# A spectral filter and a Mish network, gated, on one core: W's column copies on VectorE, four small first loads, a 128-column last piece and a new written order

## The chip, the core and the metric

The kernel runs on one core of a Trainium2 chip. Its engines work at the same time and meet only at semaphores: TensorE (PE) multiplies into PSUM, which has eight banks of 512 float32 columns; VectorE (DVE) and ScalarE (ACT) work element by element and empty PSUM; GpSimd (POOL) can do small element work in SBUF; SyncE (SP) issues the loads and stores. The metric is the time of one execution on the device, in microseconds. Three runs of the kernel before gave a median of 133.03 (132.91 to 133.15).

## What is computed

The reference, cut to what matters:

```python
x = A_x                                             # [1, 2048, 512], bf16
g = sigmoid((x * gate_w).sum(-1, keepdims=True))    # one gate for each row
a = irfft2(rfft2(x) * (A_w_r + 1j * A_w_i))         # a 2-D spectral filter, bf16
h = x @ w1 + b1                                     # [2048, 512] @ [512, 1792]
b = (h * tanh(softplus(h))) @ w2                    # Mish, then [1792, 512]
return g * a + (1 - g) * b                          # both branches read the same x
```

## The kernel before, in words

All work is cut into some 490 small tasks with names. A string, `ORDER` (L343), lists them; each engine runs its own tasks in the order in which they stand there. `place` adds what has to be waited for: the data, the former users of a buffer, and, for every load on SP, the sixth load before it (`KOUT = 6`). A task that is an engine's next but has to wait holds up everything behind it on that engine. In an entry such as `m0_0::2`, 2 is the PSUM bank (of a pair, the first); an engine name between the colons chooses the engine of tasks that have several.

The tasks that matter here, by name:

- `warm` and `fl`: products of a constant, which compute nothing that is used. `warm` is one run of `NWARM` products of 256 columns (L525); each `fl` is two products of 128 columns (L533, L534).
- `x0`, `x2`, ... load tiles of x (128 rows of 512; `XP` says which tiles one load takes). `graw` loads the gate's weights to all partitions. `w1_*`, `w2_*`, `ldM*`, `ldG*` load weights and transform matrices, `wr*s*` and `wi*s*` the filter W, `xt*` x tiles transposed by the DMA. `tr0` to `tr3` transpose the first four tiles on PE (L582), and `evx*` copy these out of PSUM.
- the spectral branch: `bf` (sums and differences of x's halves, L595, DVE), `p` (L613, PE) with eviction `ep`, `d` (L628) with `ed`, `t` (L706) with `et`; the filter, `hp`, `p1`, `ad` (L725, L728, L732, all on DVE); the edge frequencies `c0`, `e1`, `xp`, `ead`, `e2`, `e3`, of which `e3` writes into all the data that the inverse transform reads; `it` (L788) with `eit`; `id` (L827) with `ec` and `ey`.
- W's preparation, for the real and the imaginary part (`wr`, `wi`) and each half of the frequencies (0, 1): four moves `wrm000` ... `wim111` (L657, L658), a copy of one column `wrc`, `wic` (L675), a copy to the other 64 partitions, negated for the imaginary part, `wrn`, `win` (L670 on DVE, L673 on ACT), and a small fill `wrz`, `wiz` (L679).
- the gate: `gt0` to `gt15` (L602, DVE) multiply x in place and sum; `zcl`, `ez` (a power on POOL, L689), `omg`, `gc` and others make factors of it.
- the network: `m0_0` to `m3_13` (L853), four products of 512 columns each, for one of four row blocks and one of fourteen column blocks; `h0_0` to `h3_13` apply bias and Mish on ACT (L858); `h3_*` write over W's staging buffer, so they wait for all of W's moves. `ev_b` makes the bias column. `n0_0` ... `n15_0` (L871) are fourteen products each, `ip` adds the spectral branch (L879 for tiles 8 to 15, L897 for 0 to 7), `o` scales by 1 - g (L885 on ACT, L888 on DVE), `fin` adds the rest for tiles 0 to 7 (L901), `out` stores. The last tile, 15, is cut into two column pieces.

Of the kernel before, what the change touches and what calls it, by code (L numbers as in the profile page):

```python
# [340 lines left out]


ORDER = """  # L343
tab x2 ones braw cRF x0 fl9::0 w1_0 ident warm::1 bf2_0 fl6::2 tr2::3 w1_2 x4 bf2_1 evx2:dve x12 tr3::4 evx3:act w1_6 bf0_0 bf0_1 fl2::5 graw::0 p2::6
tr0::0 x8 tr1::1 w1_10 fl0::2 p3 cFD evx0:act p0::4 tr_b::3 p1 ep0:act xt7 evx1:dve m0_0::2 ev_b xt6 xt4 xt5 ep2:dve m0_1::0 m0_5::1 h0_0 ebase wr0s0
wr0s2 h0_5 bf4_0 m0_2::3 m0_3::4 h0_2 bf4_1 p4::6 wr0s1 bf12_0 bf12_1 p5 p6::1 p7 ep6:dve m0_4::5 m0_8::3 h0_3 wi0s0 ep4:act wi0s2 p14::6 gt7 p15
p12::1 p13 gt13 h0_8 h0_4 wi0s1 ep14:act m0_6::4 ep12:act bf8_1 ldM0 m0_7::3 bf8_0 p10::6 p11 gt8 xt11 ep10:act m0_13::5 gt1 h0_6 gt3 gt9 p8::1 p9
ep8:dve m0_11::6 h0_7 h0_11 gt15 m0_10::7 d0::3 gt12 h0_13 h0_10 d1 d8::1 m1_6::6 h1_6 xt10 h0_1 m1_5::5 h1_5 ldM1 m1_11::7 h1_11 d9 ed8:act ed0:dve
d12::3 d4::5 d13 xt8 gt0 gt4 d5 ed4:act m0_12::0 ed12:dve xt9 wrm010:dve d14::1 d15 wi1s0 ldM3 d2::3 d3 m1_13::7 ed14:act ed2:act h1_13 ldM2 m1_0::5
wrm000:dve h1_0 h0_12 d10::1 wr1s0 d11 ed10:act m1_1::6 m1_9::3 h1_1 wr1s1 wi1s1 m1_4::4 h1_4 xt14 h1_9 gt10 m1_3::7 h1_3 d6::1 xt13 d7 ed6:act  # L350
m1_8::5 t0::36 gt14 gt6 h1_8 gt2 et00:act xt12 et01:act m0_9::0 h0_9 m1_10::1 h1_10 gt5 xt15 t1::42 et11:act et10:act m2_9::6 h2_9 m2_12::7 h2_12
wrm001:dve m2_1::0 m2_4::1 wrm011:dve m1_2::2 h1_2 gt11 h2_4 wrc0:dve m1_7::3 h1_7 wim000:dve w2_5 m2_0::4 h2_0 wim001:dve w2_0 wrn0:dve ldG2 wrz0:dve
m2_7::5 m2_6::6 wim010:dve m2_5::7 h2_6 h2_5 m2_8::2 wim011:dve wic0:pool h2_1 m2_11::1 h2_7 win0:dve h2_8 h2_11 wiz0:pool hp00_1::1 c00 t2::36 hp00_0
hp01_1::2 hp01_0 c01 et21:act p1_00 m2_2::0 h2_2 p1_01 ad_01 hp11_0::0 hp11_1 p1_11 m1_12::5 h1_12 hp10_0::2 m2_3::2 hp10_1 ad_11 wrm100:dve et20:act
wrm110:dve h2_3 wrm111:dve wrm101:dve wim111:dve wrc1:dve t3::60 m2_13::5 et31:act m2_10::3 h2_13 wim101:dve wim110:dve wim100:dve edge et30:act
wic1:pool win1:act m3_8::4 h3_8 wrn1:dve zcl ez wrz1:pool w2_10 p1_10 ad_10 ad_00 m3_13::2 m3_1::0 wiz1:dve hp30_1::0 hp30_0 m3_12::1 ldG3 c02
m3_10::5 h3_10 h3_13 ldG0 m3_2::6 h3_12 h2_10 m3_3::7 m3_0::4 h3_0 hp20_0::2 m3_6::5 c03 p1_30 m3_11::2 hp31_1::1 m3_4::1 hp20_1 p1_20 ezb hp31_0
e1::3 p1_31 ad_31 m3_9::4 h3_1 m3_5::0 xp20::1 h3_11 xp21 n2_0::2 ad_20 h3_2 h3_6 h3_4 ad_30 h3_5 xp1::2 zt::6 ead::0 hp21_0::1 n1_0::5 hp21_1 p1_21
h3_9 zte zw ad_21 inv m3_7::1 ez1 e2::0 ldG1 n0_0::4 h3_7 e3 it4_0::0 it4_1 h3_3 rft omg o1_0:act zr o2_0:dve o0_0:act it0_0::6 it0_1 eit0:dve
it1_0::2 it1_1 eit4:dve n3_0::5 o3_0:dve it6_0::6 it6_1 eit6:act it7_0::0 it7_1 rfs eit7:act n9_0::4 eit1:dve it3_0::6 it3_1 it2_0::0 it2_1 it5_0::2  # L360
it5_1 n6_0::5 eit5:act eit2:act eit3:dve id4::6 id8::2 id9 o6_0:dve ec8:dve:2 ey8_1 ey8_0 id12::0 id13 ec12:act:0 id5 ec4:act:1 ey4_0 ey4_1 n5_0::5
o5_0:dve id6::2 id7 ec6:dve:2 id2::6 id3 ey6_1 ey12_0 ip9_0 n8_0::5 ey6_0 ec2:act:1 ip8_0 ey2_1 id14::2 ey12_1 id15 ey2_0 id0::0 id1 ec14:dve:2
o9_0:dve id10::6 o8_0:act out9 id11 ec0:dve:0 ec10:dve:1 ey10_0 n13_0::5 ey14_0 ip13_0 ey0_0 n15_256::4 ey14_1 ip15_256 o15_256:dve out15_256
o13_0:act ey10_1 ey0_1 n4_0::5 ip4::2 o4_0:act gc fin4 ip5::3 fin5 n7_0::4 ip6::6 o7_0:dve fin6 out5 ip0::7 fin0 ip2::0 ip7::1 fin7 ip1::5 fin1 out1
n14_0::2 ip3::3 ip14_0 o14_0:act out14 out7 n10_0::4 ip10_0 n11_0::6 ip11_0 o11_0:dve n12_0::7 ip12_0 n15_0::1 fin3 ip15_0 o10_0:act fl1::5 fin2 out3
fl8::2 fl4::4 o12_0:act out11 out13 fl7::6 o15_0:act out15_0 fl5::3 fl3::0
"""


def _build(nc, A_x, A_w_r, A_w_i, B_x, B_w1, B_b1, B_w2, gate_w, out, merge=8, xtp=XTP, NWARM=13):  # L370
    cs = _build_consts()
# [7 lines left out]
    G = _Graph(3)  # L379
    es = ExitStack()  # L380
    with es:
# [260 lines left out]
        for ri, (dstv, nm) in enumerate(((Wr, "wr"), (Wi, "wi"))):  # L642
            dp = t_bf + t_tr + t_gt if ri else []
            for fh in range(2):
# [27 lines left out]
                def f_dupa(e, f0=f0, dstv=dstv, sc=sc):  # L672
                    return e.activation(dstv[64:128, f0:f0 + 32, :], dstv[0:64, f0:f0 + 32, :], AF.Copy, scale=sc)  # L673

                G.add(f"{nm}c{fh}", [(g, 0.2, lambda e, dstv=dstv, f0=f0: e.tensor_copy(  # L675
                    out=dstv[0:64, f0:f0 + 32, 129], in_=dstv[0:64, f0:f0 + 32, 0])) for g in ("dve", "pool")],
                      "w", lock=True, reads=mv, writes=[(nm, fh, "c")])
# [1 line left out]
                G.add(f"{nm}z{fh}", [(g, 0.1, lambda e, dstv=dstv, ri=ri, f0=f0: e.memset(dstv[:, f0:f0 + 32, 0:1], 1.0 - ri)) for g in ("dve", "pool")],  # L679
                      "w", reads=[(nm, fh, "c")], writes=[wk])  # L680
# [164 lines left out]
        for c in range(NCH):  # L845
# [14 lines left out]

            for tl in range(4):
                t = 4 * c + tl
                for lo, hi in ([(0, 256), (256, 512)] if t == NT - 1 else [(0, 512)]):
# [13 lines left out]
                    if mg:  # L877
                        def f_ip(e, t=t, b=b, lo=lo, hi=hi):
                            return e.matmul(bank(b)[:, 0:hi - lo], RFs[:, t, :], yb[:, t, lo:hi], start=False, stop=True)  # L879
# [4 lines left out]
                    def f_oa(e, t=t, b=b, lo=lo, hi=hi):
                        return e.activation(bs[:, t, lo:hi], bank(b)[:, 0:hi - lo], AF.Copy, scale=omg[:, t:t + 1])  # L885
# [73 lines left out]
```

## Time and profile before

| | us |
|---|---|
| median of three runs | 133.03 |
| the profiled execution | 132.57 |
| its span, first to last instruction | 130.5 |
| PE busy | 124.8 |
| DVE busy | 95.3 |
| ACT busy | 69.5 |
| POOL busy | 6.2 |

The profile is of one execution. Its span leaves out about 2 us around the instructions. A row of the chain of waits gives a start, a length and what ran; a row of the groups gives line, engine, operation, tiles, shapes and count, then busy time, the mean of one in ns, and the engine's idle time before with what ended it. A matmul's listed length contains its fill and drain, which the next overlaps; what one costs in a run is the distance of two starts.

### The profile page before, as it was taken

How to read it: one execution, taken by the hardware profiler on the slowest of the kernel's cores; microseconds unless marked ns; L12 is line 12 of the kernel's file. 1: busy time of each engine (PE TensorE's matmuls, PEld its weight loads, DVE VectorE, ACT ScalarE, POOL GpSimd, SP SyncE). 2: the span in 40 equal slices, each digit the busy share in tenths (PEclk: the TensorE clock that was granted, in tenths of full speed). 3: DMA queues.
4: the chain of work that ended last, by engine and by line, in shares of the span. 5: the costliest groups of instructions: out<-in, count | busy, mean ns of one | idle time of the engine just before them, and what ended most of it. 6: DMA issues, size and time to landing. Idle time of an engine off the chain costs nothing.

```text
span 130.5 us, 2641 instructions
## 1 busy us (share of the span) xinstructions
PE 124.8 (96%) x1097; PEld 68.6 (53%) x1114; DVE 95.3 (73%) x162; ACT 69.5 (53%) x96; POOL 6.2 (5%) x12
## 2 busy tenths in 40 slices
PE   7999999999999999996999999999999999999994
PEld 5856555755554455442444454666456554444463
DVE  0758999799979999996999987734899964630230
ACT  4358798999996699959990240532212102022021
POOL 2000000000010000095000000000000000000000
PEclk9999999999999999999999999999999999999999
DMA  3899999999999791078100027000000200223024
GB/s 111 259 387 304 270 178 197 122 361 166 402 119 170 189 358 64 5 224 263 75 0 0 0 52 245 1 0 5 0 0 5 80 20 0 80 80 121 0 89 178
DMA packets 17143, 16.90 MB, mean 130 GB/s; under 512 B 7596, under 2 KB 14252, under 8 KB 17068
## 3 DMA queue, kind: packets, MB, share of 16 engines
q1 hardware_dynamic: 16960, 16.66, 53.6%
q8 instruction: 9, 0.15, 0.5%
q10 hardware_dynamic: 172, 0.07, 0.2%
q14 instruction: 2, 0.02, 0.0%
HBM read 13.05 MB, written 2.10 MB: 116 GB/s over the span
## 4 chain that ended last, share of the span: by engine, by line
PE 65%; DVE 21%; issue 4%; ACT 3%; DMA 3%; POOL 2%; SPq 1%; DVEq 0%; ACTq 0%; POOLq 0%
PE ps L871 37%; PE ps L853 15%; DVE tmp L725 4%; PE ps L788 3%; ACT rA L673 3%; DMA rA<-in_A_x_dram 3%; PE ps L613 3%; PE ps L827 2%; DVE rA L602 2%; DVE rA L658 2%; DVE rA L657 2%; DVE rW L657 2%; DVE rW L658 2%; DVE rC L728 1%; PE ps L879 1%
## 5 line engine op out<-in xcount | busy, mean ns | idle before, releaser
L853 PE MATMUL ps<-rX,w_sb 128*128 128x512 bf16 x215 | 49.5, 379 | 2.0 <-ACT rS L858 1.1
L853 PEld LDWEIGHTS ps<-rX,w_sb 128*128 128x128 bf16 x224 | 21.0, 98 | 24.8 <-ACT rS L858 1.6
L871 PE MATMUL ps<-w_sb,hs 128*128 128x512 bf16 x107 | 24.7, 379 | 0.4 <-DVE tmp L835 0.2
L885 ACT ACTIVATE rX<-ps,omg 128x512 bf16<-128x512 f32 (+1 forms) x9 | 5.9, 665 | 29.4 <-PE ps L879 23.6
L858 ACT ACTIVATE hs<-ps,b1f 128x512 bf16<-128x512 f32 x28 | 18.1, 698 | 4.1 <-PE ps L853 4.0
L871 PEld LDWEIGHTS ps<-w_sb,hs 128*128 128x128 bf16 x112 | 10.6, 98 | 12.0
L888 DVE TENSOR_SCALAR rX<-ps,omg 128x512 bf16<-128x512 f32 (+1 forms) x8 | 5.7, 716 | 14.1 <-PE ps L879 8.4
L512 ACT ACTIVATE rC<-ps 128x1024 bf16<-128x1024 f32 x13 | 13.4, 1078 | 0.6 <-PE ps L613 0.6
L871 PE MATMUL ps<-w_sb,rS 128*128 128x512 bf16 (+1 forms) x69 | 12.7, 336 | 0.2 <-issue 0.2
L871 PE MATMUL ps<-w_sb,rD 128*128 128x512 bf16 x54 | 12.6, 379 | 0.1
L858 ACT ACTIVATE rS<-ps,b1f 128x512 bf16<-128x512 f32 x14 | 8.5, 720 | 5.8 <-PE ps L853 5.8
L725 DVE TENSOR_TENSOR tmp<-rC,rA 64x1024 bf16<-64x1024 bf16 x16 | 10.9, 685 | 0.8 <-POOL rA L679 0.4
L602 DVE SCALAR_TENSOR_TENSOR rA<-rA,tmp 128x512 bf16<-128x512 bf16 x16 | 10.2, 684 | 0.2 <-DMA tmp<-in_gate_w_dram 0.2
L838 DVE TENSOR_TENSOR rA<-tmp,ps 128x512 bf16<-128x512 f32 x16 | 9.9, 680 | 0.1
L858 ACT ACTIVATE rD<-ps,b1f 128x512 bf16<-128x512 f32 x14 | 9.3, 708 | 1.2 <-PE ps L853 1.2
L732 DVE TENSOR_TENSOR rE<-rC,tmp 128x1024 bf16<-128x1024 bf16 x8 | 9.6, 1221 | 0.3
L871 PEld LDWEIGHTS ps<-w_sb,rS 128*128 128x128 bf16 x70 | 6.8, 98 | 5.6
L595 DVE TENSOR_TENSOR rB<-rA 128x1024 bf16<-128x1024 bf16 (+1 forms) x10 | 5.4, 582 | 5.3 <-DMA rA<-in_A_x_dram 5.1
L871 PEld LDWEIGHTS ps<-w_sb,rD 128*128 128x128 bf16 x56 | 5.4, 98 | 6.2
L512 ACT ACTIVATE rF<-ps 128x1024 bf16<-128x1024 f32 x4 | 3.9, 1023 | 6.6 <-PE ps L788 6.6
L901 DVE SCALAR_TENSOR_TENSOR rX<-ps,gcol,rX 128x512 bf16<-128x512 f32 x8 | 5.5, 742 | 2.1 <-ACT rX L885 2.1
L509 DVE CAST rF<-ps 128x1024 bf16<-128x1024 f32 x4 | 4.8, 1220 | 2.2 <-PE ps L788 2.2
(79 smaller groups left out, 120.2 us busy)
## 6 DMA issues: line engine op xcount, KB each, us to landing
w_sb<-in_B_w_dram SPq DMA_DIRECT2D x4, 512.0 KB, 6.5
rF<-c_m SPq DMA_DIRECT2D x4, 512.0 KB, 6.5
rB<-c_g SPq DMA_DIRECT2D x4, 512.0 KB, 6.7
out_dram<-rX SPq DMA_DIRECT2D x7, 256.0 KB, 2.1
rA<-in_A_x_dram SPq DMA_DIRECT2D x3, 512.0 KB, 6.8
w_sb<-in_B_w_dram SPq DMA_DIRECT2D x2, 640.0 KB, 6.0
rS<-in_A_w_r_dram SPq DMA_DIRECT2D x3, 257.0 KB, 7.1
rS<-in_A_w_i_dram SPq DMA_DIRECT2D x3, 257.0 KB, 5.8
```

The costliest lines, as they stand in the source:

```text
L512: return e.activation(o(), i(), AF.Copy)
L595: return e.tensor_tensor(out=xu[:, a:b_, uv, :], in0=x_sb[:, a:b_, 0:256], in1=x_sb[:, a:b_, 256:512], op=ALU.add if uv == 0 else ALU.subt ...
L602: t_gt.append(G.add(f"gt{t}", [("dve", 0.6, lambda e, t=t: e.scalar_tensor_tensor(out=x_sb[:, t, :], in0=x_sb[:, t, :], scalar=1.0, in1=tb ...
L725: return e.tensor_tensor(out=z3(z)[lo], in0=y3[hi], in1=wi3[hi], op=ALU.mult)
L732: return e.tensor_tensor(out=Yhq[:, q, h], in0=v(yv), in1=v(tb(z)), op=ALU.add)
L838: return e.tensor_tensor(out=yb[:, t:t + 2, 256 * h:256 * h + 256].rearrange("p t (i e) -> p t i e", e=2), in0=t4(z), in1=o4(bank(b, 1)), ...
L853: ins = e.matmul(bank(b), w1_sb[:, dt_, 128 * ft:128 * (ft + 1)], xT[:, c, dt_, :, :], start=(dt_ == 0), stop=(dt_ == 3))
L858: G.add(f"h{c}_{ft}", [("act", act(512, 1), lambda e, c=c, ft=ft, b=b: e.activation(hs[c][:, ft, :], bank(b), AF.Mish, bias=b1f[:, ft:ft + ...
L871: ins = e.matmul(bank(b)[:, 0:hi - lo], hs[c][:, ft, 128 * tl:128 * (tl + 1)], w2_sb[:, ft, lo:hi], start=(ft == 0), stop=(ft == NFT - 1 a ...
L885: return e.activation(bs[:, t, lo:hi], bank(b)[:, 0:hi - lo], AF.Copy, scale=omg[:, t:t + 1])
L888: return e.tensor_scalar(out=bs[:, t, lo:hi], in0=bank(b)[:, 0:hi - lo], scalar1=omg[:, t:t + 1], scalar2=None, op0=ALU.mult)
L901: return e.scalar_tensor_tensor(out=bs[:, t, :], in0=bank(b), scalar=gcol[:, t:t + 1], in1=bs[:, t, :], op0=ALU.mult, op1=ALU.add)
```

## The change

Six things change, all of them in the tasks and their order; what is computed stays.

- W's column copies and small fills can no longer be put on POOL. The copies may go to DVE or ACT; the fills are on DVE.
- The first four x tiles come in four loads of one tile instead of two loads of two, so each has its own pair of `bf` tasks, of 256 columns instead of 512.
- `NWARM` is 8 instead of 13; there are 13 fillers instead of 10.
- The last tile is cut into 128 and 384 columns instead of 256 and 256. `n15_128` and `n15_0` stand at the very end.
- `ORDER` is written anew, for all engines.
- In it the choice of engines differs: `win1` (before on ACT), `wic0` and the fills are on DVE, `wim101`, `wrm110`, `wic1` and `wrc1` on ACT.

```diff
-NFILL = 10
+NFILL = 13
-XP = ((0, 2), (2, 4), (4, 8), (8, 12), (12, 16))
+XP = ((0, 1), (1, 2), (2, 3), (3, 4), (4, 8), (8, 12), (12, 16))
...
-def _build(nc, A_x, A_w_r, A_w_i, B_x, B_w1, B_b1, B_w2, gate_w, out, merge=8, xtp=XTP, NWARM=13):
+def _build(nc, A_x, A_w_r, A_w_i, B_x, B_w1, B_b1, B_w2, gate_w, out, merge=8, xtp=XTP, NWARM=8):
...
-                G.add(f"{nm}c{fh}", [(g, 0.2, lambda e, dstv=dstv, f0=f0: e.tensor_copy(
-                    out=dstv[0:64, f0:f0 + 32, 129], in_=dstv[0:64, f0:f0 + 32, 0])) for g in ("dve", "pool")],
+                c_o, c_i = dstv[0:64, f0:f0 + 32, 129], dstv[0:64, f0:f0 + 32, 0]
+                G.add(f"{nm}c{fh}", [("dve", 0.2, lambda e, o=c_o, i=c_i: e.tensor_copy(out=o, in_=i)),
+                                     ("act", 0.2, lambda e, o=c_o, i=c_i: e.activation(o, i, AF.Copy))],
...
-                G.add(f"{nm}z{fh}", [(g, 0.1, lambda e, dstv=dstv, ri=ri, f0=f0: e.memset(dstv[:, f0:f0 + 32, 0:1], 1.0 - ri)) for g in ("dve", "pool")],
+                G.add(f"{nm}z{fh}", [("dve", 0.1, lambda e, dstv=dstv, ri=ri, f0=f0: e.memset(dstv[:, f0:f0 + 32, 0:1], 1.0 - ri))],
...
-                for lo, hi in ([(0, 256), (256, 512)] if t == NT - 1 else [(0, 512)]):
+                for lo, hi in ([(0, 128), (128, 512)] if t == NT - 1 else [(0, 512)]):
...
-                              reads=[("yb", t, h) for h in (0, 1) if lo <= 256 * h < hi] + ["RFs"], writes=[b])
+                              reads=[("yb", t, h) for h in (0, 1) if lo < 256 * h + 256 and 256 * h < hi] + ["RFs"], writes=[b])
...
-                    keys = [("bs", t, h) for h in (0, 1) if lo <= 256 * h < hi]
+                    keys = [("bs", t, lo)] if t == NT - 1 else [("bs", t, 0), ("bs", t, 1)]
```

The new order, in the parts that the prediction speaks of:

```diff
+fl8::0 tab x0 warm::1 ones ident fl7::2 fl0::3 x2 x1 bf2_1 x3 cRF w1_0 bf0_0 fl10::4 bf2_0 fl6::5 tr0::6 tr2::7 bf0_1 evx0:dve tr1::0 fl1::1 w1_2
+graw::0 x4 w1_6 x12 tr3::2 bf1_0 bf1_1 fl5::3 fl2::4 p0::5 bf3_0 p1 p2::3 evx2:dve w1_10 x8 braw tr_b::1 evx1:act bf3_1 p3 gt1 evx3:act m0_0::0 ev_b
+ep0:act gt3 ep2:act xt5 xt4 m0_1::7 bf4_0 bf4_1 h0_1 xt7 m0_4::2 xt6 h0_4 m0_5::5 h0_5 gt6 m0_2::6 h0_2 h0_0 m0_3::3 h0_3 gt4 bf12_1 p6::1 p7 m0_8::4
+p4::6 cFD p5 ep6:act xt10 h0_8 bf12_0 gt13 ep4:act m0_6::5 ldM0 m0_7::0 h0_7 p12::2 p13 ep12:act m0_12::1 gt12 h0_6 p14::6 wi0s2 p15 gt14 h0_12
...
+m1_10::3 h1_12 wim011:dve wic0:dve d4::4 d5 ed4:act xt15 h1_10 xt12 t0::06 et01:act m1_3::2 h1_3 ldM2 wi1s1 wi1s0 et00:act m2_8::4 ez win0:dve
+m2_11::5 h2_11 t1::62 wr1s0 et10:dve wr1s1 et11:act c01 m2_1::0 h2_1 w2_5 c00 wiz0 hp11_1::1 m2_13::1 w2_0 hp00_0::2 m1_6::5 h1_6 h2_13 hp11_0 hp00_1
+m1_2::2 h1_2 m2_10::3 m1_7::6 h1_7 ez1 w2_10 ldG2 m2_2::7 h2_2 h2_10 m1_11::0 wrm000:dve h1_11 m1_0::5 m2_4::1 omg ldM3 wrm001:dve t2::62 h1_0 ldG3
+et21:act et20:act m2_9::0 h2_9 m2_0::5 wrm011:dve wrm010:dve wrc0:dve h2_0 m3_3::2 hp10_1::0 hp10_0 ezb m2_5::3 h2_4 wrn0:dve wrz0 p1_00 wim101:act
+p1_10 ad_10 h2_5 m3_11::6 ad_00 m2_3::7 h2_3 wim110:dve m1_8::0 c02 h2_8 m1_1::5 h1_1 m2_7::1 h2_7 wrm110:act hp01_0::0 m3_4::3 wim100:dve hp01_1 h1_8
+p1_01 wim111:dve m3_8::7 m3_2::4 wrm101:dve m3_10::5 wrm111:dve wrm100:dve edge wic1:act win1:dve h3_8 h3_3 ldG0 ldG1 m3_1::1 h3_10 wiz1 h3_4 ad_01
+m3_5::0 h3_5 m3_12::7 wrc1:act hp20_0::2 m3_9::2 m3_7::5 h3_2 m3_0::3 h3_12 h3_0 wrn1:dve h3_11 h3_9 hp21_1::0 wrz1 p1_11 n0_0::0 hp20_1 h3_7 t3::36
+et31:act et30:act hp21_0 p1_21 ad_21 n3_0::2 o3_0:act p1_20 ad_20 m2_12::5 c03 e1::6 h3_1 ad_11 m2_6::7 h2_6 n1_0::3 o1_0:act xp20::0 xp21 xp1::2
+ead::1 e2::4 m3_13::2 hp31_0::0 hp31_1 p1_31 hp30_0::2 ad_31 m3_6::1 hp30_1 n2_0::6 h3_13 p1_30 ad_30 e3 o0_0:act h3_6 o2_0:dve it2_0::2 inv it2_1
...
+o14_0:act out14 out1 fin4 ip5::7 fin5 n13_0::0 ip12_0 o12_0:act ip3::4 fin3 out5 ip7::3 ip13_0 ip2::2 n15_128::5 ip15_128 o15_128:act n15_0::1 ip15_0
+fin2 out3 fl4::7 fin7 out7 o15_0:act o13_0:dve out13 fl9::6 fl12::4 out15_128 fl11::2 out15_0 fl3::3
```

More of the change, by code (lines that the diff above doesn't have):

```diff
@@ L343 @@
 ORDER = """
[L344 to L363, printed above, removed]
@@ new lines @@
+graw::0 x4 w1_6 x12 tr3::2 bf1_0 bf1_1 fl5::3 fl2::4 p0::5 bf3_0 p1 p2::3 evx2:dve w1_10 x8 braw tr_b::1 evx1:act bf3_1 p3 gt1 evx3:act m0_0::0 ev_b
+ep0:act gt3 ep2:act xt5 xt4 m0_1::7 bf4_0 bf4_1 h0_1 xt7 m0_4::2 xt6 h0_4 m0_5::5 h0_5 gt6 m0_2::6 h0_2 h0_0 m0_3::3 h0_3 gt4 bf12_1 p6::1 p7 m0_8::4
+p4::6 cFD p5 ep6:act xt10 h0_8 bf12_0 gt13 ep4:act m0_6::5 ldM0 m0_7::0 h0_7 p12::2 p13 ep12:act m0_12::1 gt12 h0_6 p14::6 wi0s2 p15 gt14 h0_12
+m0_13::4 h0_13 bf8_0 m0_10::0 wi0s0 bf8_1 p8::2 p9 wi0s1 ep14:act xt11 gt10 p10::4 p11 ep10:act h0_10 m0_11::1 h0_11 m1_5::6 gt9 h1_5 ep8:dve d12::2
```

10 lines of the change are left out of this document (7 added, 3 removed).

## The prediction

> **What bounds the kernel now.** I read the page first, for the busy shares.
>
> ```profile
> span 130.5 us, 2641 instructions
> PE 124.8 (96%) x1097; PEld 68.6 (53%) x1114; DVE 95.3 (73%) x162; ACT 69.5 (53%) x96; POOL 6.2 (5%) x12
> ```
>
> TensorE (PE) is busy nearly all the time, so only three things can move the end: when its unbroken run begins, how long it stands still, and what follows its last product. The chain that ended last, in order of time, gives the run, its unit prices and the one long stop:
>
> ```profile
> 7.12 4.26 PE ps L853 x19
> ...
> 16.62 0.45 PE ps L613 x8
> 17.07 0.86 PE ps L853 x4
> ...
> 55.51 1.39 POOL rA L675
> ...
> 56.99 3.67 ACT rA L673
> ...
> 127.73 0.11 PE ps L879
> ```
>
> The run starts at 7.12 (m0_0) and its last real product ends at 127.84. A block m of four products costs 0.86, two p (or d, or it) tasks 0.45, an n of 14 products 14/4 x 0.86 = 3.0. The waits of PE name its only wait above 0.8 us:
>
> ```profile
> PE ps L853 <- ACT rS L858: 1.1, 1, 1.1
> ```
>
> There PE found no free PSUM bank because ScalarE (ACT) had stood in the W chain: the column copy on POOL ended at 56.90, the 64x4160 negation on ACT ran 56.99 to 60.66, and only then came the evictions h3 (L858).
>
> The opening, from the timeline:
>
> ```profile
> 0.80 0.40 SPq L479 DMA_DIRECT2D rA<-in_A_x_dram  x1
> 1.01 2.98 PE L525 MATMUL ps<-const-bfloat16-1.0 128*128 128x256 bf16 x13
> 1.27 0.41 SPq L479 DMA_DIRECT2D rD<-c_front  x1
> 3.71 0.76 DVE L595 TENSOR_TENSOR rB<-rA 128x512 bf16<-128x512 bf16 x2 [3.71 <-DMA rA<-in_A_x_dram]
> 3.78 0.31 PE L533 MATMUL ps<-const-bfloat16-1.0 128*128 128x128 bf16 x1
> 4.73 0.22 PE L533 MATMUL ps<-const-bfloat16-1.0 128*128 128x128 bf16 x1
> 5.40 0.33 SPq L479 DMA_DIRECT2D tmp<-in_gate_w_dram  x1
> 6.37 0.33 SPq L479 DMA_DIRECT2D rA<-in_A_x_dram  x1
> 7.86 0.38 SPq L479 DMA_DIRECT2D w_sb<-in_B_w_dram  x1
> 9.14 0.33 SPq L479 DMA_DIRECT2D rD<-c_front  x1
> 10.57 4.88 SPq L478 DMA_TRANSPOSE rX<-in_A_x_dram  x3
> 13.71 0.69 DVE L602 SCALAR_TENSOR_TENSOR rA<-rA,tmp 128x512 bf16<-128x512 bf16 x1 [0.17 <-DMA tmp<-in_gate_w_dram]
> ```
>
> SP issues a load when the sixth before it has landed, so its stops are landing times: x0 near 5.40, w1_0 near 6.37, w1_2 near 7.86, x4 near 9.14, x12 near 10.57; the gate row landed at 13.7.
>
> **The change, part by part.** The products are the same, and the split 384+128 instead of 256+256 streams the same 512 columns. So the end moves by three terms.
>
> *First term, the start of the run.* Five products of 256 columns fewer: (3.78-1.01)/13 = 0.213 each, 1.07 less; three filler pairs more before the first transpose add 3 x 0.213 = 0.64 at the same slow pace. The opening run ends near 3.6 instead of 4.0. Both are cover for loads, so worth nothing in themselves. The four x loads go out at steps of 0.47 (0.80, 1.27, ...), x3 at 2.19. It lands between 5.1 (the first load's 2.9 from issue to use) and 5.4 (before, 544 KB had landed by then, now 512). Then come tr3 0.22, two filler pairs 0.22, four p tasks 0.9 and tr_b 0.1, about 6.7; w1_0, the same bytes deep in the queue, lands at 6.4. Eight subtractions and additions of 256 columns instead of four of 512 cost a little over 0.2 each on an idle VectorE (DVE). So m0_0 could start at 6.6, half a microsecond sooner. But the gate row is now issued ahead of x4, w1_6, x12 and x8. Its price: in this trace w1_6 (512 KB) and the gate row (128 KB) took 13.7-10.57 = 3.1, and 512 KB take 1.4 (9.14 to 10.57), so the gate row took 1.7, not the 0.36 of its bytes. Behind w1_2 (7.86) it lands between 8.2 and 9.6, and x4 between 9.6 and 11.0. On DVE gt1, which needs the gate row, stands ahead of ev_b (the bias all Mish evictions need), gt3 and the two bf4.
>
> ```profile
> L595 DVE TENSOR_TENSOR rB<-rA 128x1024 bf16<-128x1024 bf16 x6 | 3.9, 689 | 1.3 <-DMA rA<-in_A_x_dram 1.1
> ```
>
> From x4 at 11.0, bf4 takes two of 0.65 and ends at 12.3; p6 needs it after six m blocks, at 6.6+5.2 = 11.8. With the price this trace shows I take the late end: the half microsecond is lost at p6, and the run goes on as if it had begun at 7.1. First term 0, from -0.6 (gate row at its bytes' pace) to +0.6 (1.7 once more). I write T = 7.1. Behind p6 the loads have room: bf12 needs x12 (about 13.7) and is wanted at T+8.7 = 15.8; the four transposed loads for m1_5 end near 20.4 and are wanted at T+13.9 = 21.0.
>
> *Second term, the W chain.* The long stop goes: the negation win1 moves to DVE, the column copies leave POOL.
>
> ```profile
> L670 DVE TENSOR_SCALAR rA<-rA 64x4160 bf16<-64x4160 bf16 x1 | 1.2, 1235 | 0.5 <-POOL rA L675 0.5
> L675 POOL COPY rA<-rA 64x32 bf16<-64x32 bf16 x2 | 1.7, 850 | 47.1 <-DVE rA L658 30.4 <-DVE rA L657 16.7
> L675 DVE COPY rW<-rW 64x32 bf16<-64x32 bf16 x2 | 0.5, 228 | 0.0
> L725 DVE TENSOR_TENSOR tmp<-rC,rA 64x1024 bf16<-64x1024 bf16 x16 | 10.9, 685 | 0.8 <-POOL rA L679 0.4
> L728 DVE TENSOR_TENSOR rC<-rC,rW 128x1024 bf16<-128x1024 bf16 x8 | 5.4, 689 | 0.2
> L732 DVE TENSOR_TENSOR rE<-rC,tmp 128x1024 bf16<-128x1024 bf16 x8 | 9.6, 1221 | 0.3
> L658 DVE TENSOR_SCALAR rW<-rS 32x2064 bf16<-32x2064 bf16 x4 | 2.7, 696 | 0.1
> 47.65 1.07 PE L706 MATMUL ps<-rE,rF 32*128 32x128 bf16 x64
> 48.88 2.54 PE L853 MATMUL ps<-rX,w_sb 128*128 128x512 bf16 x11 [0.16 <-issue]
> ```
>
> A t task costs 1.23 (47.65 to 48.88). In the new order t1 ends after 23 m blocks, 28 p or d tasks and two t: 19.8+6.3+2.5 = T+28.6 = 35.7. Eviction et10 now stands on DVE ahead of everything for W and the filter, and DVE, done with wi0, has nothing to do before it for some 2 us. With 1.2 for et10 it starts its list at 37.0. From there to e1's result: 12 hp at 0.72, 10 W moves at 0.72, three negations or copies wn at 1.27, six p1 at 0.70, six ad at 1.24, and 1.7 for the four c0, wrc0 and seven tiny ones at 0.1 to 0.3, the gaps of 0.03 included: 8.6+7.2+3.8+4.2+7.4+2.2 = 33.4, so 70.4. Three joins hang on this list.
>
> (a) h3 may start only after the last W move (wrm100), 20.5 into the list: 57.5. ACT gets there in time: m2_7 ends at T+46.2 = 53.3, h2_7 0.7 (as the eviction of the same size in the ACT row of L885 below), wrm110 on ACT 1.8 (the 4160-element ACT row 3.67, halved; up to 3.67 undiminished), h1_8 0.7, wic1 about 0.3 (0.23, the DVE row, to 1.39, POOL's dearer one in the chain): 56.8. h3_8 ends at 58.2, PE wants its bank for m3_12 at T+51.4 = 58.5. No stall, 0.3 to spare. (b) win1 waits for wic1 (56.8, wanted 57.5), wrn1 for wrc1, which stands on ACT behind h3_5: both in time, the second just. (c) e1 ends at T+63.2 = 70.3, DVE reaches it at 70.4; then xp20, xp21, xp1 and ead 1.5, four hp, two p1, two ad 6.75, e3 0.45: 79.1. The inverse stage it2 needs e3 and PE is there at T+71.8 = 78.9: a new stop of 0.2.
>
> Second term: -1.13+0.2 = -0.9. Bounds: -1.13 if DVE keeps up; +2.6 with the dearest rows for ACT's moves and column copies (wic1 2.2 late and wrc1 another 1.3, counted as in the third rival).
>
> *Third term, the end.* The last eviction has 128 columns instead of 256.
>
> ```profile
> L885 ACT ACTIVATE rX<-ps,omg 128x512 bf16<-128x512 f32 x8 | 5.4, 688 | 28.4 <-PE ps L879 22.7 <-PE ps L871 4.0 <-DVE omg L692 1.8
> L885 ACT ACTIVATE rX<-ps,omg 128x256 bf16<-128x256 f32 x1 | 0.5, 476 | 0.9 <-PE ps L879 0.9
> out_dram<-rX ACTq DMA_DIRECT2D x1, 64.0 KB, 1.6
> scz<-rD SPq DMA_DIRECT2D x1, 4.0 KB, 1.3
> rD<-c_front SPq DMA_DIRECT2D x1, 32.0 KB, 2.6
> ```
>
> By the two rows 128 columns cost 0.37, so 0.1 less. The store now has 256-byte rows: 1.3 (the small store with such rows) to 2.6 (a load of 128 such rows behind another), against 1.6; I keep 1.6, as it is the same queue and half the bytes. out15_128 leaves SP when o15_128 is done, 0.6 before out15_0, behind out13, and is no later. The closing fillers run beside it. Third term -0.1, from -0.4 to +0.9. The Trainium skill, "DMA: Bandwidth & Descriptors", Specifications, puts rows under 512 bytes to a read-modify-write, which speaks against this piece; no row here shows it at this size, and with the longest row (2.6) the whole gain of the change would be gone.
>
> Sum: 0-0.9-0.1 = -1.0. The profiled execution took 132.57 (span 130.5 and 2.07 around it), 0.46 under the median of the runs, 133.03. So 131.6 as profiled, **132.0** as a median.
>
> **Rivals.** *First, the opening keeps its half microsecond.* If the gate row lands at its bytes' pace, p6 waits for nothing and T is 6.6; the joins (a) to (c) move with t1. 132.0-0.5 = 131.5. Against it: 1.7 for that row in the trace.
>
> *Second, the clock opens late and nothing is left.* Two 128-column products of the opening run are 0.107 apart by the 13 of 0.213, eight from 16.62 on 0.056 each, and between 4.0 (two products after 3.78) and 4.73 eight transposes took 0.7: TensorE reached its full pace there, after some 3.5 us without a pause. The new dense run is 0.4 shorter and then has transposes that wait for one x tile each. If the full pace comes one such stretch later, near 8.1, the 3.5 us in between run at half pace: 1.75 lost, of which the 0.5 that p6 waits anyway is no loss. 132.0+1.2 = 133.2, no change. For it: nothing but that run; against it: the transposes are work too and p tasks follow at once. The Trainium skill, "TensorE: Matmul & The Clock Gate", Part 1, says that a free-running window of 3.4 us must be busy, and Part 4 that transposes do not count as such; by that rule this rival's condition is met whenever the window's end falls as in this trace.
>
> *Third, slower: ACT's W work makes DVE the bound.* Its place is wic1 and wrc1. Neither a half W move nor a column copy on ACT is in the trace. If a move costs 2.75, midway between 1.8 and 3.67, and a column copy 1.39, wic1 ends at 53.3+0.7+2.75+0.7+1.39 = 58.8 and DVE's win1 is 1.3 late; then five evictions at 0.6 to 0.7 and wrc1 end near 63.3, where DVE wants it at 58.8+1.27+0.1+1.24+0.72 = 62.1, 1.2 late again. e3 and it2 come 2.4 later: 132.0+2.4 = 134.4. It decides from 1.0 us of lateness on. For it: the list has no slack at (b) and (c), and DVE stands idle before et10. Against: ACT's time in the row is 0.88 ns an element.
>
> **How the numbers follow.** Forecast 0.52 (own range 131.5 to 132.6), first rival 0.13, second 0.13, third 0.18, other 0.04, half of it faster. The range leaves out the best of the first rival and the third with the dearest rows: 130.9 to 134.4. Under 0.2% (0.27 us) is what a measurement of this kernel cannot tell from no change; forecast and first rival are faster, the second is same, the third slower: 0.67, 0.13, 0.20.
>
> **What would show it.** Right: no POOL copy in the chain; PE's wait for ACT h3 (1.1) gone; the gate row landing well over 0.4 after w1_2 and a PE wait at p6 for DVE's bf4; DVE idle before et10 and full from there to e3; a short PE wait for e3 at it2. Wrong: no wait at p6 and a run that starts by 6.7 without loss (first rival); 128-column products still 0.107 apart after 5 us (second); ACT copies of 32x2064 well over 1.9 us, DVE waiting for ACT at win1 or wrn1 and PE over 1 us at it2 (third); a last store over 2 us.

## The result, and the profile after

| | before | after |
|---|---|---|
| median of the runs, us | 133.04 (22 runs, 132.63 to 133.39) | 132.63 (22 runs, 131.86 to 133.71) |
| ratio, with its 95% interval | | 0.9963 [0.9947, 0.9979] |
| the profiled execution, us | 132.57 | 132.26 |
| its span, us | 130.5 | 130.1 |

The change made the kernel faster by 0.37%, or 0.4 us; the forecast was 1.0. The runs of the changed kernel also lie further apart, 1.9 us from lowest to highest instead of 0.8. Medians and ratios below leave out runs that took over 1.5% longer than the fastest of their kernel, at a lower granted clock: one of a_graw_late and two of a_graw_o13.

PE's waits in the changed kernel (engine, line, what it waited for; us in total, times, longest). Its lines stand one or two further down than in the kernel before, from W's copies on:

```profile
PE ps L533 <- PEq L945: 0.8, 1, 0.8
PE ps L872 <- issue: 0.5, 3, 0.2
PE ps L854 <- issue: 0.3, 2, 0.2
PE ps L789 <- DVE rE L776: 0.3, 1, 0.3
```

The 1.1 us for ACT's h3 are gone, and the new wait at it2 (L789) for e3 (L776) is there. The opening, from the timelines of PE, its weight loads (PEld) and DVE:

```profile
5.47 0.31 PE L533 MATMUL ps<-const-bfloat16-1.0 128*128 128x128 bf16 x1
5.58 0.31 PE L534 MATMUL ps<-const-bfloat16-1.0 128*128 128x128 bf16 x1
...
6.84 0.40 PE L613 MATMUL ps<-rD,rB 128*128 128x128 bf16 x4
7.29 5.13 PE L854 MATMUL ps<-rX,w_sb 128*128 128x512 bf16 x23
...
9.51 0.69 DVE L602 SCALAR_TENSOR_TENSOR rA<-rA,tmp 128x512 bf16<-128x512 bf16 x1 [3.73 <-DMA tmp<-in_gate_w_dram]
...
10.83 1.29 DVE L595 TENSOR_TENSOR rB<-rA 128x1024 bf16<-128x1024 bf16 x2
...
12.17 0.52 PEld L613 LDWEIGHTS ps<-rD,rB 128*128 128x128 bf16 x8 [0.25 <-DVE rB L595]
12.26 0.61 PE L613 MATMUL ps<-rD,rB 128*128 128x128 bf16 x8
```

The gate row lands at 9.5, gt1, the bias and gt3 fill DVE to 10.8, bf4 runs to 12.1, and p6 goes at 12.26. Only a weight load waits for bf4 there. PE's own products run on without a pause, and no row of PE's waits stands at p6. The chain that ended last, in order of time, now passes through the gate row: its load is the first long piece.

```profile
4.16 5.33 DMA tmp<-in_gate_w_dram
9.48 0.02 issue
9.51 0.70 DVE rA L602 x2
10.21 0.10 DVE b1f L574
...
127.06 0.06 PE ps L880
```

The W chain, from the timelines of DVE, ACT and PE:

```profile
35.82 1.23 DVE L509 CAST rC<-ps 128x1024 bf16<-128x1024 f32 x1 [1.90 <-PE ps L707]
...
54.24 1.93 ACT L655 ACTIVATE rW<-rS 32x2064 bf16<-32x2064 bf16 x1
56.78 0.33 ACT L677 ACTIVATE rA<-rA 64x32 bf16<-64x32 bf16 x1
57.21 1.24 DVE L670 TENSOR_SCALAR rA<-rA 64x4160 bf16<-64x4160 bf16 x1 [0.17 <-ACT rA L677]
...
78.65 0.44 DVE L776 CAST rE<-ps 128x64 bf16<-128x64 f32 x1
...
79.15 1.29 PE L789 MATMUL ps<-rB,rE 128*128 128x128 bf16 x20 [0.26 <-DVE rE L776]
```

And the end, from the timelines of SP and ACT and the list of transfers (KB each, median us from issue to landing):

```profile
124.67 0.33 SPq L479 DMA_DIRECT2D out_dram<-rX  x1
125.33 0.33 SPq L479 DMA_DIRECT2D out_dram<-rX  x1
126.03 0.81 SPq L479 DMA_DIRECT2D out_dram<-rX  x1
126.92 0.39 SPq L479 DMA_DIRECT2D out_dram<-rX  x1
127.15 0.37 ACT L886 ACTIVATE rX<-ps,omg 128x128 bf16<-128x128 f32 x1 [0.26 <-PE ps L880]
127.55 0.38 ACTq L479 DMA_DIRECT2D out_dram<-rX  x1
...
out_dram<-rX ACTq DMA_DIRECT2D x1, 32.0 KB, 2.1
```

In the kernel before, SP's last store and the last store of all left like this:

```profile
126.96 0.33 SPq L479 DMA_DIRECT2D out_dram<-rX  x1
128.39 0.38 ACTq L479 DMA_DIRECT2D out_dram<-rX  x1
```

The last store now leaves at 127.55 with four others behind one another in the three microseconds ahead of it, and takes 2.1 us, where it took 1.6.

The three terms of the forecast can be read off a trace. The first record of the dense run is often missing, so its start T is taken back from the first p behind it: p6 less six blocks (12.26 - 6 x 0.863 = 7.08); in the kernel before p4 less five (11.22 - 4.31 = 6.91). What PE waits between the first block and that p counts in T. The second term is the time from T to the end of the last real product in the chain (127.12; before, 127.84), the third what is left of the span.

```
                     forecast   before   after   difference
start T                  0        6.91    7.08     +0.17
T to last product      -0.9     120.93  120.04     -0.89
what follows           -0.1       2.63    2.96     +0.33
sum                    -1.0     130.47  130.08     -0.39
```

The second term came out as forecast. The third has the wrong sign. The first is off because the forecast had read the start before as 7.12: that row of the chain has 19 products where five blocks have 20, so the run began one product earlier, at 6.91.

### The profile page after: what moved, and what is told of

The parts are those of the page before. It is cut to its first block, busy times and chain, and to the rows that moved or that the text cites. A ratio compares the mean times of both kernels' runs of the same rounds, so it can differ in the third digit from the quotient of the medians.

```text
span 130.1 us, 2649 instructions
## 1 busy us (share of the span) xinstructions
PE 125.1 (96%) x1099; PEld 69.2 (53%) x1115; DVE 93.3 (72%) x163; ACT 72.3 (56%) x103; POOL 4.7 (4%) x8
## 4 chain that ended last, share of the span: by engine, by line
PE 74%; ACT 8%; DVE 7%; DMA 4%; SPq 2%; issue 2%; ACTq 0%; DVEq 0%
PE ps L872 33%; PE ps L854 27%; ACT hs L859 5%; DMA tmp<-in_gate_w_dram 4%; PE ps L828 3%; PE ps L789 3%; PE ps L628 3%; SPq L479 2%; PE ps L707 2%; ACT rC L512 2%; DVE tmp L726 2%; DVE rE L733 2%; PE ps L898 1%; PE ps L880 1%; DVE rC L729 1%
## 5 line engine op out<-in xcount | busy, mean ns | idle before, releaser
L886 ACT ACTIVATE rX<-ps,omg 128x512 bf16<-128x512 f32 (+2 forms) x10 | 6.4, 644 | 30.4 <-PE ps L880 21.9
L512 ACT ACTIVATE rC<-ps 128x1024 bf16<-128x1024 f32 x14 | 14.7, 1088 | 3.2 <-PE ps L707 2.8
L872 PE MATMUL ps<-w_sb,rS 128*128 128x512 bf16 (+2 forms) x69 | 12.9, 336 | 0.1
L872 PEld LDWEIGHTS ps<-w_sb,rS 128*128 128x128 bf16 x70 | 6.3, 98 | 6.1
L889 DVE TENSOR_SCALAR rX<-ps,omg 128x512 bf16<-128x512 f32 x7 | 5.2, 748 | 4.4 <-PE ps L880 3.0
L595 DVE TENSOR_TENSOR rB<-rA 128x256 bf16<-128x256 bf16 (+1 forms) x14 | 5.7, 458 | 3.5 <-DMA rA<-in_A_x_dram 3.4
L509 DVE CAST rF<-ps 128x1024 bf16<-128x1024 f32 x5 | 6.0, 1217 | 1.8 <-PE ps L789 1.6
L512 ACT ACTIVATE rF<-ps 128x1024 bf16<-128x1024 f32 x3 | 3.0, 1022 | 7.2 <-PE ps L789 7.2
```

Of the source, the lines that this page charges most:

```text
L509: return e.tensor_copy(out=o(), in_=i())
L512: return e.activation(o(), i(), AF.Copy)
L595: return e.tensor_tensor(out=xu[:, a:b_, uv, :], in0=x_sb[:, a:b_, 0:256], in1=x_sb[:, a:b_, 256:512], op=ALU.add if uv == 0 else ALU.subt ...
L872: ins = e.matmul(bank(b)[:, 0:hi - lo], hs[c][:, ft, 128 * tl:128 * (tl + 1)], w2_sb[:, ft, lo:hi], start=(ft == 0), stop=(ft == NFT - 1 a ...
```

## The experiments

Each was timed beside the kernel before on the same chip; ratios are to that. Kernels whose names begin with b start from the kernel before, those with a from the changed one. The table has the three lengths of the table above, for the profiles of these kernels and for a second profile of the changed one (after_again). It also has the time at which the trace's record of the granted clock goes to full, the start of the first gate product, which waits for the gate row (in a_tail_graw2 it stands behind bf12 besides), and the beginning of the dense run itself, where a missing first product is added. T less this beginning is what PE lost ahead of p6:

```
                 clock full   gate row   run       start T   T to last   what
                                         begins              product     follows
before               4.59       13.71     6.91       6.91     120.93      2.63
b_copies             5.66         -       7.51       7.51     120.23      2.63
b_copies_again       3.49         -       6.23       6.23     120.15      2.62
b_copies_win         6.29         -       7.52       7.52     121.11      2.63
b_last128            4.69         -       6.85       6.85     121.24      2.69
after                6.03        9.51     7.08       7.08     120.04      2.96
after_again          5.37        9.76     7.09       7.26     120.11      3.62
a_split256           3.76       10.48     6.64       7.95     120.13      3.07
a_no_out7_13         4.00        9.83     7.29       7.31     120.13      2.39
a_o13_act            5.71        9.48     6.93       7.08     120.03      2.81
a_tail             no record     9.74     7.10       7.25     120.12      2.40
a_graw_late          6.40       14.12     7.26       7.26     121.76      3.45
a_tail_graw2         5.15       14.85     6.67       6.67     121.42      2.40
```

### The W chain

**b_copies**: the kernel before, with only two column copies and two fills moved from POOL to DVE.

```diff
-... wic0:pool ... wiz0:pool ... wic1:pool ... wrz1:pool ...
+... wic0:dve ... wiz0:dve ... wic1:dve ... wrz1:dve ...
```

> The kernel before with one part of the change alone: both column copies of wi and the two small fills that were on POOL go to VectorE; the negation win1 stays on ScalarE, the order stays. Theory (the stop of 1.1 us on TensorE before m3 came from the slow POOL copy and the negation behind it, and VectorE had an idle microsecond there): the copy takes 0.23 instead of 1.39, win1 starts near 55.8 instead of 57.0, the stop shrinks to 0 to 0.2, VectorE's list to e3 gets about 0.8 shorter because its wait for win1 (1.0) ends earlier; time 0.7 to 0.9 us under before. Rival (the end of VectorE's list at e3 decides, and one more copy lengthens it): time within 0.2 us of before, the stop moved to the first it task.

Measured: 132.28 us, ratio 0.9938 [0.9917, 0.9960]. **b_copies_again** is the same kernel on another chip:

> The kernel before with only the first rows' column copies and memsets (wic0, wic1, wiz0, wrz1) on VectorE, once more, on the chip of the two others. As before, 0.6 to 0.8 us under the kernel before; by the theory that the two differ only in the start and the end, level with a_tail within 0.3 us.

Measured: 132.11 us, ratio 0.9945 [0.9923, 0.9968]. PE's waits of b_copies:

```profile
PE ps L533 <- PEq L944: 0.8, 1, 0.8
PE ps L853 <- issue: 0.6, 4, 0.2
PE ps L788 <- DVE omg L692: 0.4, 1, 0.4
...
```

The long wait is gone as in the changed kernel, a shorter one at the first inverse product (L788) has come, and the stretch from T to the last product is 0.7 and 0.8 shorter. Nothing else was changed, and the whole change did no better: 0.9938 and 0.9945 here, against 0.9963 and, measured again further down, 0.9988. So most of the second term stands by itself, and what the other edits brought together was no gain and rather a loss. The intervals of single measurements overlap, so its size is open.

**b_copies_win**: win1 on DVE as well.

```diff
-... win1:act ...
+... win1:dve ...
```

> As the one above, and the negation win1 goes to VectorE too, as in the change, in the old order. If only the stop before m3 counts: 1.1 us under before. If VectorE's list to e3 decides: the stop before m3 is gone, but copy and negation add 1.5 to VectorE where it had 1.0 of idle time, e3 ends near 77.6 instead of 77.05 and TensorE, which comes to the first it task 1.1 earlier, waits there 1.5 or more: time 0.3 to 0.6 us above before.

Measured: 133.41 us, ratio 1.0026 [1.0012, 1.0040]. PE's waits, the ones that grew:

```profile
PE ps L788 <- DVE omg L692: 0.7, 1, 0.7
...
PE ps L769 <- DVE tmp L762: 0.3, 1, 0.3
```

In the old order DVE's list up to e3 has no room for 1.24 us more: the end comes 0.9 later than in b_copies. The changed kernel can carry win1 on DVE, as its order has it, because two of W's moves left DVE's list in exchange (0.70 us each there, 1.92 on ACT). That is read from the lists; no run took only these moves back.

### The end

**a_split256**: the last tile in halves of 256, at the places of the new order.

```diff
-... [(0, 128), (128, 512)] if t == NT - 1 ...
+... [(0, 256), (256, 512)] if t == NT - 1 ...
```

> The changed kernel with the last tile cut 256+256 as before, all else as changed. In the changed kernel's profile the last store took 2.07 from issue to landing, not 1.6. If its 256-byte rows are slow: with 512-byte rows it takes 1.6, the store is issued 0.1 later, and the time is 0.35 us under the changed kernel. If it is late because out13 and the other piece were issued 1.5 and 0.6 us ahead of it on the same DMA engines: 1.9 to 2.1 again, and the time is 0 to 0.15 us above the changed kernel.

Measured: 132.75 us, ratio 0.9983 [0.9964, 1.0002]. Its last store, with rows of 512 bytes, takes as long as that of the changed kernel with rows of 256:

```profile
out_dram<-rX ACTq DMA_DIRECT2D x1, 64.0 KB, 2.1
```

So the length of the rows is not what makes it long.

**a_no_out7_13**: the stores of tiles 6, 7, 12 and 13 are left out; their values are computed and evicted.

```diff
-... fin7 out7 ... o13_0:dve out13 ...
+... fin7 ... o13_0:dve ...
```

> The changed kernel without two of the stores just ahead of the end: tiles 6, 7, 12 and 13 are computed and not stored. If the last store is late because of those: 1.6 from issue to landing, 0.4 to 0.5 us under the changed kernel. If its 256-byte rows are slow: 2.0 to 2.1 still, and the time within 0.1 us of the changed kernel.

Measured: 132.12 us, ratio 0.9935 [0.9914, 0.9956]. The same last store, with the same rows:

```profile
out_dram<-rX ACTq DMA_DIRECT2D x1, 32.0 KB, 1.5
```

Two stores fewer ahead of it and it takes 1.5. This is the pile-up, and the packets in the traces show it. Here the 256-byte packets of the last store run from 128.74 to 129.01, with all others done by 128.52. In the changed kernel they run from 128.44 to 129.16, and beside them the 96 KB piece goes on until 129.04 and tile 13 until 128.77. The rule that the prediction drew from the Trainium skill, "DMA: Bandwidth & Descriptors", Specifications (below 512 bytes there is a read-modify-write), makes no store late here: 256-byte rows that go alone land no later than the 512-byte rows of the kernel before (1.6).

**a_o13_act**: tile 13 evicted on ACT and its store ahead of those of tiles 3 and 7.

```diff
-... ip13_0 ip2::2 ... o13_0:dve out13 ...
+... ip13_0 o13_0:act out13 ip2::2 ...
```

> The changed kernel with the eviction of tile 13 on ScalarE right behind its product (ScalarE is idle from 123.70 to 126.31 us), instead of on VectorE behind three others, and the store of tiles 12 and 13 issued right behind it, ahead of those of tiles 3 and 7. Theory (four stores in the last 3 us queue on the same DMA engines): the store's issue goes from 126.03 to about 124.5, the last store takes 1.5 to 1.6 us from issue to landing instead of 2.07, and the median is 0.35 to 0.5 us under the changed kernel's. Rival (the last store is long because its rows are 256 bytes): it still takes 2.0 to 2.1 us, and the median stays within 0.1 us.

Measured: 132.70 us, ratio 0.9992 [0.9969, 1.0015], beside the changed kernel's second measurement:

> The changed kernel once more, for a second profile of it on the chip of the three that follow. If the landing of x4 sets the start of the dense run (theory), the span of this profile differs from the first one's 130.1 us by as much as the first product behind bf4_1 (line 613, 12.26 us in the first profile) differs: it may lie anywhere from 12.2 to 13.2, as it did in the two kernels with the same opening (12.49 and 13.13). If the clock's opening sets it (rival), the span follows the time at which the clock opens instead. The last store takes 2.0 to 2.1 us from issue to landing again. Median 132.4 to 132.8.

132.66 us, ratio 0.9988 [0.9966, 1.0011]: taken alone, this second measurement of the change cannot be told from no change. a_o13_act is a miss: the last store of a_o13_act still takes 1.9 us, and the median has not moved. The order was not enough. The store of tile 13 did leave at 124.35, but now that of tile 7 was the one held, issued from 125.31 to 126.73. In the second profile of the changed kernel the store of tile 13 was held even longer, and the 96 KB piece, which leaves SP after it, became the last to land:

```profile
126.27 1.53 SPq L479 DMA_DIRECT2D out_dram<-rX  x1
127.85 0.43 SPq L479 DMA_DIRECT2D out_dram<-rX  x1
...
out_dram<-rX SPq DMA_DIRECT2D x1, 96.0 KB, 2.7
```

What follows the last product is 3.62 us in this execution, 1.0 more than before. Its span is 0.9 longer than in the first profile, while p6 comes only 0.2 later (12.44 for 12.26); most of the rest is this end. In each profile with a held issue, a 16 KB transfer of instructions was under way at that moment, and the issue ended shortly after it (times from the trace's packets):

```
                instructions       held store      after the transfer
before          125.38 to 126.32   until 126.68         0.36
b_copies        125.32 to 126.53   until 126.89         0.36
b_copies_again  123.97 to 125.02   until 125.40         0.38
b_last128       126.40 to 127.36   until 127.73         0.37
after           125.44 to 126.61   until 126.84         0.23
after_again     125.75 to 127.44   until 127.80         0.36
a_split256      126.20 to 127.45   until 127.82         0.37
a_o13_act       125.39 to 126.57   until 126.73         0.16
a_graw_late     127.29 to 128.87   until 129.24         0.37
```

**a_tail** keeps every store out of that stretch: the products of tiles 3, 2 and 7 go ahead of those of tile 13, so that three of the four late stores leave earlier.

```diff
-... ip5::7 fin5 n13_0::0 ip12_0 o12_0:act ip3::4 fin3 out5 ip7::3 ip13_0 ip2::2 n15_128::5 ...
+... ip5::7 fin5 ip3::4 fin3 out5 ip2::2 fin2 out3 ip7::3 fin7 out7 n13_0::0 ip12_0 o12_0:act ip13_0 o13_0:act out13 n15_128::5 ...
-fin2 out3 fl4::7 fin7 out7 o15_0:act o13_0:dve out13 fl9::6 ...
+fl4::7 o15_0:act fl9::6 ...
```

> The changed kernel with the products of tiles 3, 2 and 7 moved ahead of those of tile 13, so that their stores leave before 123.5 us, and tile 13 evicted on ScalarE as in a_o13_act: of the four late stores one (tiles 12 and 13, issued near 124.4) is left ahead of the two pieces of tile 15, and no store is being issued while instructions are fetched at 125.4 to 126.6. Theory (stores still under way lengthen the last one): it takes 1.5 to 1.6 us from issue to landing, as in a_no_out7_13, and the median is 0.4 to 0.6 us under the changed kernel's, 132.0 to 132.25. Rival (no pile-up, the store's length is chance): 1.9 to 2.7 us again, and the median within 0.1 us of 132.65.

Measured: 131.94 us (131.68 to 132.58), ratio 0.9950 [0.9925, 0.9975].

```profile
122.12 0.33 SPq L479 DMA_DIRECT2D out_dram<-rX  x1
122.78 0.33 SPq L479 DMA_DIRECT2D out_dram<-rX  x1
125.20 0.33 SPq L479 DMA_DIRECT2D out_dram<-rX  x1
127.17 0.33 SPq L479 DMA_DIRECT2D out_dram<-rX  x1
127.80 0.38 ACTq L479 DMA_DIRECT2D out_dram<-rX  x1
...
out_dram<-rX ACTq DMA_DIRECT2D x1, 32.0 KB, 1.5
```

No issue takes longer than 0.4, the last store takes 1.5, and 2.40 us follow the last product. The median lies 0.7 under both measurements of the changed kernel, more than the 0.56 between the ends of the first profiles (2.96 and 2.40), as it should be if other executions of the changed kernel end like its second profile. The runs lie within 0.9 us again, though there are only nine. By ratios, which were taken on different chips, the gain over the changed kernel is 0.1% to 0.4% with overlapping intervals. So the shorter end is shown in the profiles (2.40 here, in a_no_out7_13 and in a_tail_graw2), and its worth in the median only roughly.

**b_last128**: the 128-column cut alone, in the old order.

```diff
-... [(0, 256), (256, 512)] if t == NT - 1 ...
+... [(0, 128), (128, 512)] if t == NT - 1 ...
```

> The kernel before with one edit only: the last output tile cut at column 128 instead of 256, so that its early piece has 384 columns and the last piece 128; nothing else moves in the order. The last piece's fourteen products take about 0.9 us instead of 1.7, so the products and stores ahead of it come about 0.8 us later, nearer to the last store. Theory (stores still under way lengthen the last one): its issue comes 0.1 us earlier by the shorter eviction, and it takes 1.8 to 2.1 us instead of 1.61, so the median is 0.1 to 0.4 us above the kernel before. By the third term as predicted: the store stays at 1.6 and the median is 0.1 us under it.

Measured: 133.29 us, ratio 1.0011 [0.9992, 1.0029]. The store takes 1.8, behind another one issued half a microsecond earlier instead of 1.4:

```profile
out_dram<-rX ACTq DMA_DIRECT2D x1, 32.0 KB, 1.8
```

The shorter last eviction and the longer store cancel at the end (2.69 against 2.63). The cut alone brings nothing that can be measured; a gain of 0.1 us is at the edge of the interval. T to the last product is 0.3 longer in its profile; no run asked why.

### The start

**a_graw_late**: the gate row behind x4, w1_6 and x12, and the gate products gt1 and gt3 behind bf4.

```diff
-graw::0 x4 w1_6 x12 tr3::2 ...
+x4 w1_6 x12 graw::0 tr3::2 ...
-... gt1 ... gt3 ... bf4_0 bf4_1 h0_1 ...
+... bf4_0 bf4_1 gt1 gt3 h0_1 ...
```

> The changed kernel with the load of the gate row issued behind x4, w1_6 and x12 instead of ahead of them, and the two gate products that need it (gt1, gt3) put on VectorE behind bf4_1 instead of ahead of it. Theory (the gate row's 128 KB hold up x4, which holds the first product behind bf4_1): x4 lands about 1.7 us earlier, near 9.1 to 9.4, bf4_1 ends near 10.5, the product at line 613 no longer waits, and the dense run is limited by its own start: 0.3 to 0.5 us under the changed kernel's median, so 132.1 to 132.3, with a narrower spread. Rival (the shorter opening run opens the clock later and that sets the start): within 0.1 us of the changed kernel. Second rival (x4's place only passes the delay on to w1_10 or x8): within 0.1 us, with a new wait for a load between 12 and 20 us.

Measured: 134.49 us (five runs), ratio 1.0141 [1.0102, 1.0180]: slower than the changed kernel by 1.8 us, which no theory had. From its PE waits and its DVE timeline:

```profile
PE ps L613 <- DVE rB L595: 1.8, 1, 1.8
...
9.92 1.29 DVE L595 TENSOR_TENSOR rB<-rA 128x1024 bf16<-128x1024 bf16 x2 [2.62 <-DMA rA<-in_A_x_dram]
14.12 0.69 DVE L602 SCALAR_TENSOR_TENSOR rA<-rA,tmp 128x512 bf16<-128x512 bf16 x1 [2.90 <-DMA tmp<-in_gate_w_dram]
```

x4 is there at 9.92, and in the changed kernel its last packet landed at 10.80: 0.9 earlier, not 1.7, so the gate row costs x4 about half of its price in the trace of before. And DVE, which had worked off gates and bf4 between 9.5 and 13.4, now stands still between bf4 and 14.1; then four gates come ahead of bf12, and PE waits for that. **a_graw_o13** is this with the edit of a_o13_act:

> Both of the two edits before. The start and the end of the kernel have nothing in common, so by both theories the gains add: 0.65 to 1.0 us under the changed kernel, 131.6 to 132.0. If only the end counts, 132.1 to 132.3.

Measured: 134.64 us (four runs), ratio 1.0163 [1.0114, 1.0212], a miss for the same reason; PE stops at the same place. **a_tail_graw2** has the late row in a_tail, with the four gates behind bf12 too:

```diff
-... bf12_1 p6::1 p7 ... h0_8 bf12_0 gt13 ...
+... bf12_0 bf12_1 p6::1 p7 ... h0_8 gt1 gt3 gt6 gt4 gt13 ...
```

> The kernel before this one with the gate row's load behind x4, w1_6 and x12, as in a_graw_late, but with the gate products gt1, gt3, gt6 and gt4 behind bf12_1 and bf12_0 on VectorE, so that no product of TensorE stands behind the row's landing. Theory (in a_graw_late it was the gate products ahead of bf12 that stopped TensorE for 1.8 us): that stop is gone, p12 no longer waits, and the median is 0 to 0.3 us under a_tail's, since the start is then set by the dense run's own beginning (6.4 to 7.3 us), no longer by x4. Rival (the row is late for something else too): a new wait of TensorE for VectorE before 20 us, and slower than a_tail by as much.

Measured: 132.66 us, ratio 0.9977 [0.9952, 1.0001], 0.7 above a_tail. The stop has only moved on, to the p that needs bf8, as the rival had it:

```profile
20.48 1.07 PE L613 MATMUL ps<-rD,rB 128*128 128x128 bf16 x16 [1.50 <-DVE rB L595]
```

T is 6.67 there, early as hoped, and 1.3 us are lost afterwards. The early row can cost something at p6 and is worth more behind it: it gives DVE its gates while x12 is still on its way.

The table of lengths answers what sets T. With the old opening nothing is lost ahead of p4, and T follows the clock: 6.23, 6.91, 6.85, 7.51, 7.52 for a clock that is full at 3.49, 4.59, 4.69, 5.66, 6.29 (in b_copies, the 7.51, PE also waited 0.3 for w1). With the new one T is the later of two things. The first is the beginning of the run. Where PE waits for nothing there, this too comes later with a later clock: 6.67, 6.93, 7.08, 7.26 for 5.15, 5.71, 6.03, 6.40. In after_again and a_no_out7_13 PE waited for w1 instead (0.2 and 1.0). The second is bf4: with the early row p6 comes 2.6 to 2.8 us behind the row's landing in all six profiles. In five of these the two lie so close together that 0.2 at most is lost at p6. Only a_split256 shows a long wait there:

```profile
6.86 5.12 PE L854 MATMUL ps<-rX,w_sb 128*128 128x512 bf16 x23
13.13 0.62 PE L613 MATMUL ps<-rD,rB 128*128 128x128 bf16 x8 [1.15 <-DVE rB L595]
```

Its clock was the earliest of the six, 3.76, and its gate row the latest, 10.48. The clock itself does not follow the opening run: with 13 products it was full between 3.5 and 6.3, with 8 between 3.8 and 6.4.

## Why the prediction was half right

- **Direction and cause** were right, the size was not: 0.4 instead of 1.0.
- **Second term**: as predicted, -0.89 for -0.9. The joins held as worked out: et10 at 35.82 (35.8) after 1.90 of idle time; ACT's moves of 32x2064 took 1.92 and 1.93 (1.8) and its column copy 0.33 (0.3); win1 started at 57.2 (57.5); PE resumed at 79.15 (79.1). The third rival's condition was not met by any of its rows (DVE waited 0.17 for wic1 ahead of win1), and b_copies shows most of the term alone.
- **Third term**: the step that failed is the sentence that kept the last store at 1.6 "as it is the same queue and half the bytes", and let out15_128 be "no later" without asking what SP had still to send. It measured +0.33 in the first profile and +1.0 in the second, for -0.1. The new order puts out3, out7, out13 and two pieces of tile 15 in the last three microseconds; a_no_out7_13 and a_tail show that with these stores out of the way the same piece lands in 1.5, and the term would have been -0.23. The range given for it, up to +0.9, took in the first profile and was bounded by the wrong thing, the length of rows.
- **First term**: 0 was predicted, +0.17 measured. T = 7.1 came out to the tenth, but by another way, and that was luck. The forecast was a run that begins at 6.6, with w1_0 landed at 6.4, and loses half a microsecond at p6. In the profile the run began at 7.08 and lost nothing at p6. The clock, full only at 6.03, set that beginning; w1_0, landed at 6.72, would have allowed one near 6.85, going by the 0.14 from landing to product in a_split256 (6.50, 6.64). The sign that was named for it, a wait of PE at p6, is missing. The gate row, gt1 and bf4 came as worked out, so they would have held up a run that began at 6.6, as in a_split256 (6.64, then 1.3 lost). But w1_0 landed between 6.1 and 7.15 in these six profiles, so such an early start is itself rare. What made 0 into +0.17 is the start before, read as 7.12 instead of 6.91. And this is one execution of several. Over the profiles with each opening T averages 7.00 for the old (five) and 7.32 for the new (six), so the new opening may cost some 0.3; T scatters by 1.3 within the old five, so that is a rough estimate.
- **First rival** (the opening keeps half a microsecond): a_split256 began that early and lost it at p6; T below 6.7 occurred with the late row and was lost to DVE. **Second rival** (the clock opens late): the condition was met, fillers are 0.11 apart until 5.9. The price came as at most half a microsecond, the beginning at 7.08 instead of 6.6, because the full pace came at 6.03 and not at the assumed 8.1; it took the place of the wait at p6. The old opening's clock is no more reliable. The Trainium skill, "TensorE: Matmul & The Clock Gate", Part 1, calls the window free-running and puts the variation from run to run at half a microsecond either way. The traces agree with the first: the full clock lasts 126.29 us in eleven of the twelve records of the table and 129.71 in the other, 37 and 38 times 3.413, wherever it begins. They show more than the second, 2.9 us between the earliest and the latest. They also speak for the transposes counting as work, if each such stretch is judged by itself: in a_graw_late the stretch from 2.99 to 6.40 opened the clock with 1.7 us of transposes and 1.7 of other products, and the one before it, with 2.2 of products, did not.

One slip in the working of the second term does no harm: it lists 1.7 us of small tasks and adds 2.2. With 1.7, e1's end at 70.3 would have been the later of the two, and e3 0.1 earlier.

The sum in medians: the second term of -0.9, less about 0.3 at the start and 0.3 or more at the end, leaves a few tenths. Why the runs lie further apart stays open. The held store moves the end by 0.7 between the two profiles of the changed kernel, and the runs of a_tail, without it, lie closer. But T scatters no more with the new opening (0.9) than with the old (1.3), and the runs of b_copies_again, with the old opening and the old end, lie 1.35 us apart.

The best version here is the changed kernel with a_tail's order, 131.94 us, beside b_copies, the old order with four small tasks moved, at 132.11 on the same chip; the two cannot be told apart (0.9950 and 0.9945).

## What to carry to other kernels

When an order is written anew, list what each DMA queue has still to send when the last store is issued: even a smaller last piece lands later if stores that could have left earlier are still under way. A load that looks too early for its own consumer may be what keeps another engine busy while the next load arrives, so move it only with the list of that engine at hand. One profile is one draw: where the start hangs on a clock or a landing, compare several before a tenth is believed, and check the way to a number that came out right: here a late clock stood in for the wait that had been forecast.

## What had not been expected of the hardware

- An issue of a store on SP that met a 16 KB transfer of instructions took 0.8 to 1.5 us instead of 0.33 to 0.45 and ended 0.16 to 0.38 us after that transfer, in all nine profiles in the table above. That the transfer is the cause was not tried; in a_tail, which moves the stores away from it, no issue was held.
- The clock became full between 3.49 and 6.40 us after the first instruction, whatever the opening run, and stayed full for a multiple of 3.413 us.
